# Query turns tile by tile, and an earlier, more spread image chain, in a fused attention and ReGLU kernel

## The chip, the cores and the metric

The kernel runs on one core of a Trainium2 chip. The metric is the device time of one execution in microseconds (us), taken as the median of several runs. The core has a matrix engine (TensorE, PE in the profile; its weight loads are PEld), three engines for element work (VectorE = DVE, ScalarE = ACT, GpSimd = POOL), and a sequencer that mostly issues transfers (SyncE = SP). Each engine works its own instructions in order.

## The reference

Attention over a spatially reduced image, followed by a gated feed-forward layer. There are 4 batches of 12288 queries, C = 128 channels, and an image of 384 x 32 pixels per batch, which is averaged in 4 x 4 blocks to 768 keys. Keys and values are the same numbers.

```python
kv_pool = kv.reshape(B, H // r, r, W // r, r, C).mean(axis=(2, 4))   # r = 4
k = v = kv_pool.reshape(B, -1, C) @ w_sr                             # 768 x 128 per batch
s = (q @ k.transpose(0, 2, 1)) / np.sqrt(C)
a = np.exp(s - s.max(-1, keepdims=True))
a /= a.sum(-1, keepdims=True) + 1e-09
x = (a @ v).reshape(B * N, C)
gate = np.maximum(x @ w_gate, 0.0)                                   # d_ff = 1536
out = (gate * (x @ w_val)) @ w_out
```

All inputs and the output are float32; the kernel computes in fp16 with sums in float32.

## The kernel before

The 49152 queries are cut into 96 tiles of 512. Four tiles make a group (24 groups), 24 tiles make a batch. After an opening that does the scores of tiles 0 to 3 in a special order, a loop runs over k = 4 to 98. In step k the kernel works on several tiles at once: the scores of tile k (`score_block`, `exp_block`), the values of tile k - 2 (`values`, `keep_values`), the two hidden projections of tile k - 3 (`value_proj`, `gate_proj`), and the output projection of tile k - 4 (`out_proj`, `out_turn`). The order inside a step is written out by hand as a list of words (`STEADY` and its fellows); nothing is reordered later. In what follows "tile k" is also the name of the loop's step k.

In a step of the steady state TensorE has 8 score matmuls, 6 value matmuls (L399) and 36 matmuls of the feed-forward part. The exponentials of a tile are made by ScalarE in four pieces of 128 queries (L362). They come out with queries on the partitions, but the value matmul wants keys there, so each piece is turned by a transposing transfer, `a_turn` (L389), into the tile `aT`, issued on SP right after its exponential in the word order. Step k + 2 reads it. Four `aT` tiles exist.

Queries are loaded by group on POOL's queue (`q_load`, four transfers with a cast to fp16, into one of two `q16` buffers) and turned by one transposing transfer of 16 blocks on SP (`q_turn`, L154) into one of three `qT` buffers. With ph = k % 4, both stand at ph = 1: the turn of group g + 1 and then the load of group g + 2. An older function, `q_turn_tile` (L193), turns one tile alone (4 blocks) and is used in the opening.

Keys and values of batches 1 to 3 are made while the batch before is computed, by `image_step` and three words of the list. The 768 keys come in three pairs of 128-key chunks. For each pair, with `since` counted in steps:

- four loads of image lines on SP, two per step (`kv_load`, L223, 512 KB each, two buffers `kv_in`),
- the block sums on POOL, one half of the pair per step (`pool_pixels`, L233 to L241),
- the word `tb`: a block turn on VectorE, its store to DRAM on SP (L321), and in the same step four reads from there on SP (L712), which wait for the store to land,
- the words `P` and `pk`: the projection with w_sr on TensorE and the kept keys on VectorE,
- two transposing transfers on SP, which make the values from the keys (`turn_values_dma`, L332).

A pair starts four steps after the one before.

Output stores are issued alternately on POOL's and SP's queue in the step after `out_turn` (L736): four transfers per tile, but sixteen small ones per tile for the first group, which are issued in steps 5 to 8.

So SP's queue holds, in program order: the `aT` turns, the query turns, half of the output stores, the image loads, the block store and reads, and the value turns. A transfer that has to wait for something holds up all that stand behind it.

Of the kernel before, what the change touches and what calls it, by code (L numbers as in the profile page):

```python
# [10 lines left out]
FP16 = mybir.dt.float16  # L11
# [5 lines left out]
def kernel(  # L17
# [23 lines left out]
    nc = tc.nc  # L41

    B, N, C = q.shape
# [8 lines left out]
    NS = T // 128  # L52
    NST = N // T
    NT = B * NST
    GRP = 4
# [45 lines left out]
    work = ctx.enter_context(tc.tile_pool(name="work", bufs=2))  # L101
# [19 lines left out]
    q16s, qTs, q32s, q_banks = {}, {}, {}, {}  # L121
# [11 lines left out]
    def q_load(g):  # L133
        if not 0 <= g < NG:
            return
        b, n0 = divmod(g * GRP * T, N)
        q16 = work.tile([128, GRP * NS, C], FP16, tag="q16", bufs=2)
        rows = q[b, n0 : n0 + GRP * T, :]
        if g == NG - 1:
            nc.gpsimd.dma_start(q16, rows.rearrange("(p s) c -> p s c", p=128))  # L140
        else:
            rows = rows.rearrange("(i t j s) c -> j t i s c", i=GRP, t=32, s=NS)
            for j in range(4):
                nc.gpsimd.dma_start(  # L144
                    q16[32 * j : 32 * (j + 1)].rearrange("t (i s) c -> t i s c", i=GRP), rows[j]
                )
        q16s[g] = q16

    def q_turn(g):
        if not 0 <= g < NG:  # L150
            return
        q16 = q16s.pop(g)
        qT = work.tile([128, GRP * NS, 128], FP16, tag="qT", bufs=3)
        nc.sync.dma_start_transpose(qT, q16.rearrange("p s c -> p (s c)"))  # L154
        qTs[g] = qT

    def q_load_pair(i):
        q32 = work.tile([128, 2, NS, C], FP32, tag="kv_s2", bufs=2, name="q32")
# [44 lines left out]
    kv16 = const.tile([128, B, NJC, 2 * C + 16], FP16)  # L203
    kv_in = {}

    def kv_load(b, pair, lines=range(r), queues=(nc.sync,)):
        if (b, pair) not in kv_in:
            if (b, pair) == (0, NJC // 2 - 1):
                kv_in[b, pair] = [
                    work.tile([128, NS * J // 2], FP32, tag="a16", bufs=4, name="kv_line")[  # L210
                        :, 0 : 2 * r * C
                    ].rearrange("p (h dw c) -> p h dw c", h=2, dw=r)
                    for dh in range(r)
                ]
            else:
                lines_in = work.tile([128, r, 2, r, C], FP32, tag="kv_in", bufs=2, name="kv_in")
                kv_in[b, pair] = [lines_in[:, dh] for dh in range(r)]
        parts = kv_in[b, pair]
        rows = kv[b, pair * 2 * HC : (pair + 1) * 2 * HC].rearrange(
            "(hp dh) (wp h dw) c -> dh hp wp (h dw c)", dh=r, h=2, dw=r  # L220
        )
        for dh in lines:
            queues[dh % len(queues)].dma_start(  # L223
                parts[dh].rearrange("p h dw c -> p (h dw c)"), rows[dh]
            )
# [3 lines left out]
    def pool_pixels(eng, b, pair, h):  # L229
        parts = kv_in[b, pair]  # L230
        s2 = work.tile([128, 2, r, C], FP32, tag="kv_s2", bufs=2)
        for i in range(2):
            eng.tensor_tensor(s2[:, i], parts[2 * i][:, h], parts[2 * i + 1][:, h], op=ALU.add)  # L233
        s1 = work.tile([128, r, C], FP32, tag="kv_s1", bufs=2)
        eng.tensor_tensor(s1, s2[:, 0], s2[:, 1], op=ALU.add)
        c2 = work.tile([128, 2, C], FP32, tag="kv_c2", bufs=2)
        eng.tensor_tensor(c2, s1[:, 0:2], s1[:, 2:4], op=ALU.add)
        if h == 0:
            s3s[b, pair] = work.tile([128, 4, 2, 32], FP32, tag="kv_s3", bufs=2, name="kv_s3")
        c4 = c2.rearrange("p i (j c) -> p i j c", c=32)  # L240
        eng.tensor_tensor(s3s[b, pair][:, :, h], c4[:, 0], c4[:, 1], op=ALU.add)  # L241
# [85 lines left out]
            for j in range(4)  # L327
        ]

    def turn_values_dma(b, pair):  # L330
        for jc in (2 * pair, 2 * pair + 1):
            nc.sync.dma_start_transpose(kv16[:, b, jc, C : 2 * C], kv16[:, b, jc, 0:C])  # L332


    aTs, x_banks, x16s, xTs, rinvs = {}, {}, {}, {}, {}
    hTs, o_banks, o_sbs, vals = {}, {}, {}, {}
# [41 lines left out]
    def spread_scales(k, j):  # L378
        if j == 0:
            scales[k // 2] = work.tile([128, 2, NS * 4], FP32, tag="scale", bufs=3, name="scale")  # L380
        to = scales[k // 2].rearrange("t e (s j) -> t e s j", j=4)
        for b in range(4):
            nc.gpsimd.tensor_copy(  # L383
                to[32 * b : 32 * (b + 1), :, :, j], squares[k // 2][32 * j : 32 * (j + 1)]
            )
# [99 lines left out]
    def out_proj(k, fb):  # L485
        if k >= NT - 3:
            if fb == 0:
                o_banks[k] = bank([128, NS, 128])
            for s in range(NS):
                out_add(k, fb, s, o_banks[k][:, s, :], fb == 0 and s == 0)  # L490
            return
        if fb == 0:
            o_banks[k] = bank([128, T])
        nc.tensor.matmul(  # L494
            o_banks[k], wo16[:, fb, :], hTs[k][:, fb, :], start=fb == 0, stop=fb == NFB - 1
        )
# [205 lines left out]
    out_moves, moves, spread = [], [], []  # L702

    def image_step(b, at, step):
        for pair in range(NJC // 2):
            since = at - 4 * pair
            if since in (0, 1) and step in (2, 8):
                kv_load(b, pair, [2 * since + step // 8])
            elif since in (2, 3) and step == 3:
                pool_pixels(nc.gpsimd, b, pair, since - 2)  # L710
            elif since == 5 and moves and step > 4:
                nc.sync.dma_start(*moves.pop())  # L712
            elif since == 8 and step == 1:
                turn_values_dma(b, pair)

    last = NT + LAG - 1
    for k in range(LEAD, last + 1):
        g, ph = divmod(k, GRP)
        if k == GRP:
            nc.sync.dma_start_transpose(  # L720
                qTs[1][:, 2 * NS :], q16s.pop(1)[:, 2 * NS :].rearrange("p s c -> p (s c)")
            )
        if ph == 1:
            q_turn(g + 1)
            q_load(g + 2)
        b = k // NST + 1
        at = k % NST - 6
        kO, kF, kV = k - LAG - 1, k - LAG, k - 2
        words = FIRST if kV < LEAD else STEADY if k < NT else DRAIN if k < last else LAST
        for word in words:  # L730
            head, n = word.rstrip("0123456789"), int(word.lstrip("abcdefghijklmnopqrstuvwxyzADPT") or 0)
            if head == "o":
                out_proj(kO, n)
                for queue in (nc.gpsimd, nc.sync):
                    if out_moves and n >= 2:
                        queue.dma_start(*out_moves.pop())  # L736
                if spread:
                    spread_scales(*spread.pop(0))
                if b < B:
                    image_step(b, at, n)  # L740
            elif head == "oT":
                if kO < NT - 3:
                    out_moves = out_turn(kO)
                elif k < last:
                    out_scale(kO, nc.vector, slice(0, NS))
                    out_store(kO, slice(0, NS))
            elif head in ("v", "y", "g", "h"):
                if kF < NT:
                    {"v": value_proj, "y": keep_value, "g": gate_proj, "h": gated}[head](kF, n)
            elif head in ("s", "e"):  # L750
                if k < NT:
                    {"s": score_block, "e": exp_block}[head](k, n)
                    if head == "e":
                        a_turn(k, n, n + 1)
            elif head == "r":
                if LEAD < k <= NT and k % 2 == 0:
                    invert(k - 2)
                    spread += [(k - 2, j) for j in range(4)]
            elif head in ("tb", "P", "pk"):
                pair, since = divmod(at - 5 if head == "tb" else at - 7, 4)  # L760
                if b < B and 0 <= pair < NJC // 2 and since == 0:
                    if head == "tb":
                        moves.extend(turn_blocks(b, pair))
                    elif head == "P":
                        project(b, pair)
                    else:
                        keep_projected(b, pair)
            elif LEAD <= kV < NT:
                if head == "x":
                    values(kV, n)  # L770
                else:
                    keep_values(kV)
# [33 lines left out]
```

The softmax here doesn't subtract the row's maximum and nothing guards it: scores larger than these inputs give would overflow.

## Time and profile before

| What | us |
| --- | --- |
| median of 5 runs | 1035.7 |
| lowest and highest run | 1033.78, 1037.03 |
| the profiled execution: its time | 1034.61 |
| the profiled execution: its span | 1032.8 |
| PE busy | 1022.4 |
| ACT busy | 921.0 |
| DVE busy | 862.7 |
| POOL busy | 524.5 |

The mean granted clock of the profiled execution is 0.997. The profile is of one execution: the span runs from its first to its last instruction, and its time is 1.8 us longer. Matmuls are pipelined, so PE's busy time counts overlapping instructions once. In a timeline line the first number is the start in us from the span's start, the second the length, then the engine (SPq is SP's queue of transfers, where the length is the time that issuing took, not the time until the data landed), the source line, the operation and the tiles (written<-read). In brackets stands the idle time of the engine before it, and what ended it. A line of the waits reads: who waited, for whom, us in total, times, longest.

### The profile page before, as it was taken

What the parts mean: (1) busy time and instruction counts of PE and PEld (TensorE: products, weight loads), DVE (VectorE), ACT (ScalarE), POOL (GpSimd) and SP (SyncE); (2) the same over time, 40 slices, a digit from 0 to 9 for tenths busy, and PEclk for the clock granted to TensorE, in tenths of its full rate; (3) what the DMA queues carried; (4) which work ended last, traced back from release to release, by engine and by line L of the source; (5) the groups of instructions that cost most, each with busy time, mean ns of one, the idle gap of its engine ahead of it and who ended that gap; (6) DMA issues with size and microseconds to landing.
All of it is one profiled execution on the core that took longest, in us unless ns stands there. A gap on an engine that the chain in (4) does not pass through costs nothing.

```text
span 1032.8 us, 18011 instructions
## 1 busy us (share of the span) xinstructions
PE 1022.4 (99%) x5048; PEld 490.0 (47%) x5048; DVE 862.7 (84%) x1432; ACT 921.0 (89%) x1931; POOL 524.5 (51%) x1308
## 2 busy tenths in 40 slices
PE   9999998999999999999999999999999999999998
PEld 5444443444444444444444444444444444444445
DVE  2888887788888888888888888888888888888888
ACT  5999997799999999998999999989899999999986
POOL 3576473843544656565433666566343543343332
PEclk9999999899999999999999999999999999999999
DMA  9998998997979989898888898997996876856541
GB/s 329 129 162 156 172 169 176 138 157 130 154 128 198 154 173 166 154 140 145 139 146 143 183 185 152 180 139 130 148 161 123 138 122 127 143 105 120 103 85 45
DMA packets 480500, 153.55 MB, mean 149 GB/s; under 512 B 456720, under 2 KB 470544, under 8 KB 480400
## 3 DMA queue, kind: packets, MB, share of 16 engines
q1 hardware_dynamic: 458368, 126.10, 67.0%
q0 software_dynamic: 21600, 25.19, 15.8%
q10 hardware_dynamic: 432, 1.11, 0.3%
q8 instruction: 40, 0.66, 0.3%
q14 instruction: 60, 0.49, 0.2%
HBM read 53.94 MB, written 26.35 MB: 78 GB/s over the span
## 4 chain that ended last, share of the span: by engine, by line
PE 96%; DMA 2%; ACT 1%; DVE 0%; issue 0%; SPq 0%; DVEq 0%
PE bank_ps L453 24%; PE bank_ps L466 24%; PE bank_ps L494 23%; PE bank_ps L399 12%; PE wide_ps L357 11%; DMA aT<-a 1%; DMA q<-in_q_dram 1%; PE bank_ps L480 1%; PE bank_ps L342 1%; PE bank_ps L416 1%; PE wide_ps L298 0%; PE bank_ps L266 0%; DVE hT L474 0%; ACT a L362 0%; PE bank_ps L280 0%
## 5 line engine op out<-in xcount | busy, mean ns | idle before, releaser
L474 DVE SCALAR_TENSOR_TENSOR hT<-bank_ps,val 128x512 f16<-128x512 f32 x1152 | 728.7, 680 | 110.4 <-PE bank_ps L466 88.8
L460 ACT CAST val<-bank_ps 128x512 f16<-128x512 f32 x1149 | 628.8, 596 | 46.9 <-PE bank_ps L453 26.7
L453 PE MATMUL bank_ps<-xT,wv 128*128 128x512 f16 x1152 | 421.2, 380 | 0.0
L466 PE MATMUL bank_ps<-xT,wg 128*128 128x512 f16 x1152 | 376.4, 379 | 0.0
L494 PE MATMUL bank_ps<-hT,wo 128*128 128x512 f16 x1116 | 348.4, 379 | 0.0
L362 ACT ACTIVATE a<-wide_ps 128x768 f16<-128x768 f32 x368 | 302.0, 821 | 49.8 <-PE wide_ps L357 49.7
L399 PE MATMUL bank_ps<-aT,kv 128*128 128x512 f16 x552 | 180.3, 382 | 5.2 <-DMA aT<-a 4.8
L357 PE MATMUL wide_ps<-kv,qT 128*128 128x512 f16 x736 | 180.1, 326 | 0.1
L494 PEld LDWEIGHTS <-wo 128*128 128x128 f16 x1116 | 109.2, 98 | 131.7 <-issue 0.3
L466 PEld LDWEIGHTS <-wg 128*128 128x128 f16 x1152 | 112.8, 98 | 121.9
L453 PEld LDWEIGHTS <-wv 128*128 128x128 f16 x1152 | 112.9, 98 | 106.2 <-issue 2.2
L507 POOL TENSOR_TENSOR o_sb<-o_t,scale 128x512 f32<-128x512 f32 x89 | 93.4, 1049 | 134.5 <-issue 119.2
L383 POOL COPY scale<-square 32x8 f32<-32x8 f32 x736 | 141.4, 192 | 28.6
L736 POOL DMA_DIRECT2D out_dram<-o_sb x216 | 134.7, 627 | 18.8 <-POOL o_sb L507 13.0
L357 PEld LDWEIGHTS <-qT 128*128 128x128 f16 x736 | 72.1, 98 | 87.5 <-issue 0.9
L376 POOL TENSOR_TENSOR square<-inverse 128x8 f32<-128x8 f32 x46 | 9.5, 206 | 202.0 <-DVE inverse L374 202.0
L407 DVE CAST xT<-bank_ps 128x512 f16<-128x512 f32 x92 | 63.6, 692 | 34.1 <-PE bank_ps L399 34.1
L399 PEld LDWEIGHTS <-kv 128*128 128x128 f16 x552 | 54.3, 98 | 72.6 <-DMA aT<-a 6.6
L233 POOL TENSOR_TENSOR s<-kv_in 128x512 f32<-128x512 f32 x36 | 45.5, 1272 | 74.7 <-DMA kv_in<-in_kv_dram 74.0
L362 ACT ACTIVATION_READ_ACCUMULATOR a<-wide_ps 128x1 f32 x368 | 75.9, 206 | 0.0
L502 DVE STREAM_TRANSPOSE o_t<-bank_ps 128x512 f32<-128x512 f32 x93 | 65.5, 704 | 0.0
L144 POOL DMA_DIRECT2D q<-in_q_dram x84 | 46.7, 574 | 0.4 <-PE bank_ps L494 0.4
(78 smaller groups left out, 205.2 us busy)
## 6 DMA issues: line engine op xcount, KB each, us to landing
kv_in<-in_kv_dram SPq DMA_DIRECT2D x42, 512.0 KB, 4.6
out_dram<-o_sb SPq DMA_DIRECT2D x177, 64.0 KB, 2.2
out_dram<-o_sb POOLq DMA_DIRECT2D x176, 64.0 KB, 3.2
q<-in_q_dram POOLq DMA_DIRECT2D x84, 128.0 KB, 5.5
aT<-a SPq DMA_TRANSPOSE x368, 3.4
kv_line<-in_kv_dram SPq DMA_DIRECT2D x4, 512.0 KB, 9.7
placed<-blocks SPq DMA_DIRECT2D x9, 128.0 KB, 3.4
kvT<-placed SPq DMA_DIRECT2D x36, 32.0 KB, 1.9
```

The costliest lines, as they stand in the source:

```text
L357: nc.tensor.matmul(s_ps[:, j0 * 128 : j1 * 128], qT, kv16[:, b, j0:j1, 0:C], start=True, stop=True)
L362: nc.scalar.activation(a16s[k][:, s, :], s_banks.pop(s)[:, 0:J], AF.Exp, scale=qk_scale, accum_out=a_sums[k // 2][:, k % 2, s : s + 1],)
L383: nc.gpsimd.tensor_copy(to[32 * b : 32 * (b + 1), :, :, j], squares[k // 2][32 * j : 32 * (j + 1)])
L399: nc.tensor.matmul(x_banks[k], kv16[:, k // NST, jc, C : 2 * C], aT[:, jc], start=first, stop=x_left[k] == 0,)
L453: nc.tensor.matmul(proj_banks["v", k, fb], wv16[:, fb * 128 : (fb + 1) * 128], xTs[k], start=True, stop=True,)
L460: (nc.vector.tensor_copy if k < LEAD - 1 and fb == 5 else nc.scalar.copy)(vals[k, fb], freed(proj_banks.pop(("v", k, fb))))
L466: nc.tensor.matmul(proj_banks["g", k, fb], wg16[:, fb * 128 : (fb + 1) * 128], xTs[k], start=True, stop=True,)
L474: nc.vector.scalar_tensor_tensor(hTs[k][:, fb, :], freed(proj_banks.pop(("g", k, fb))), 0.0, vals.pop((k, fb)), op0=ALU.max, op1=ALU.mult,)
L494: nc.tensor.matmul(o_banks[k], wo16[:, fb, :], hTs[k][:, fb, :], start=fb == 0, stop=fb == NFB - 1)
L502: nc.vector.transpose(o_t, freed(o_banks.pop(k)))
L507: nc.gpsimd.tensor_tensor(to, o_by, scale.to_broadcast([128, NS, 4, 32]), op=ALU.mult)
L736: queue.dma_start(*out_moves.pop())
```

## The change

Four edits.

1. `q_turn` takes a tile number i and turns only that tile's 4 blocks. The first three tiles of group g + 1 are turned at ph = 1, 2 and 3 of group g, the last at ph = 0 of its own group, each at the start of the step. The load of group g + 2 stays at ph = 1; its buffer is that of group g, whose last part is now read by the turn issued one step before.
2. The image chain begins two steps sooner: `at` is k % 24 - 4 instead of - 6.
3. Within the chain, the sums come at since 3 and 4 instead of 2 and 3, the reads and `tb` at 6 instead of 5, `P` and `pk` at 8 instead of 7. With the sooner begin, the loads stand two steps earlier than before and all of these one step earlier.
4. The two value turns of a pair stand at since 9 and 11, one each, instead of both at 8.

The same instructions are issued as before, except that each query turn of 16 blocks has become four of 4 blocks.

```diff
-    def q_turn(g):
+    def q_turn(g, i):
         if not 0 <= g < NG:
             return
-        q16 = q16s.pop(g)
-        qT = work.tile([128, GRP * NS, 128], FP16, tag="qT", bufs=3)
-        nc.sync.dma_start_transpose(qT, q16.rearrange("p s c -> p (s c)"))
-        qTs[g] = qT
+        if g not in qTs:
+            qTs[g] = work.tile([128, GRP * NS, 128], FP16, tag="qT", bufs=3, name="qT")
+        at = slice(i * NS, (i + 1) * NS)
+        nc.sync.dma_start_transpose(
+            qTs[g][:, at], q16s[g][:, at].rearrange("p s c -> p (s c)")
+        )
+        if i == GRP - 1:
+            del q16s[g]
...
-    def turn_values_dma(b, pair):
-        for jc in (2 * pair, 2 * pair + 1):
-            nc.sync.dma_start_transpose(kv16[:, b, jc, C : 2 * C], kv16[:, b, jc, 0:C])
+    def turn_values_dma(b, jc):
+        nc.sync.dma_start_transpose(kv16[:, b, jc, C : 2 * C], kv16[:, b, jc, 0:C])
...
             since = at - 4 * pair
             if since in (0, 1) and step in (2, 8):
                 kv_load(b, pair, [2 * since + step // 8])
-            elif since in (2, 3) and step == 3:
-                pool_pixels(nc.gpsimd, b, pair, since - 2)
-            elif since == 5 and moves and step > 4:
+            elif since in (3, 4) and step == 3:
+                pool_pixels(nc.gpsimd, b, pair, since - 3)
+            elif since == 6 and moves and step > 4:
                 nc.sync.dma_start(*moves.pop())
-            elif since == 8 and step == 1:
-                turn_values_dma(b, pair)
+            elif since in (9, 11) and step == 1:
+                turn_values_dma(b, 2 * pair + since // 11)
...
+        if ph == 0 and g > 1:
+            q_turn(g, GRP - 1)
+        elif ph > 0:
+            q_turn(g + 1, ph - 1)
         if ph == 1:
-            q_turn(g + 1)
             q_load(g + 2)
         b = k // NST + 1
-        at = k % NST - 6
+        at = k % NST - 4
...
-                pair, since = divmod(at - 5 if head == "tb" else at - 7, 4)
+                pair, since = divmod(at - 6 if head == "tb" else at - 8, 4)
```

## The prediction

> **What bounds the kernel now.** I read the page's busy times first, then PE's waits, then the timelines around the longest wait.
>
> ```profile
> PE 1022.4 (99%) x5048; PEld 490.0 (47%) x5048; DVE 862.7 (84%) x1432; ACT 921.0 (89%) x1931; POOL 524.5 (51%) x1308
> ```
>
> TensorE is at work for 99% of the span, and the change removes no matmul. So it can only win back idle TensorE time, or add some. The waits of PE after the opening are these:
>
> ```profile
> PE bank_ps L399 <- DMA aT<-a: 4.8, 2, 4.3
> PE bank_ps L399 <- DVE o_t L502: 0.4, 1, 0.4
> ```
>
> Three waits, all in front of the value matmuls (L399), which read the turned weights aT. The longest in PE's timeline, with the granted clock around it in the windows view (PEclk is the column behind POOL's):
>
> ```profile
> 175.86 0.38 PE L453 MATMUL bank_ps<-xT,wv 128*128 128x512 f16 x1
> 180.54 0.59 PE L399 MATMUL bank_ps<-aT,kv 128*128 128x512 f16 x1 [4.30 <-DMA aT<-a]
> ...
> 176.00:179.60 3.60, 0.24 (x2) 0.00 (x0) 1.21 (x2) 0.79 (x2) 1.12 (x1) 1.00 1.15 212
> 179.60:186.40 6.80, 5.86 (x15) 2.63 (x16) 2.08 (x3) 2.40 (x5) 6.48 (x13) 0.50 0.87 153
> 186.40:196.80 10.40, 10.40 (x52) 4.87 (x51) 8.57 (x15) 8.89 (x20) 9.55 (x22) 1.00 1.24 158
> ```
>
> TensorE stands still from 176.24 to 180.54, and the clock is at half for 6.8 us from 179.6 on. What the tile paid is read from DVE's output turn (L502), one per tile:
>
> ```profile
> 165.52 0.69 DVE L502 STREAM_TRANSPOSE o_t<-bank_ps 128x512 f32<-128x512 f32 x1
> 175.92 0.72 DVE L502 STREAM_TRANSPOSE o_t<-bank_ps 128x512 f32<-128x512 f32 x1
> 194.10 0.69 DVE L502 STREAM_TRANSPOSE o_t<-bank_ps 128x512 f32<-128x512 f32 x1
> ```
>
> A tile takes 10.37 (10.34 and 10.39 in turn), 10.82 where an image pair is projected. This one took 194.10 - 175.92 = 18.18, so 7.36 too much. The two small ones (475.22 to 486.62, 725.86 to 737.32) took 11.40 and 11.46, 0.6 too much each. All other tiles run at TensorE's pace. **The change can win 7.36 + 0.59 + 0.64 = 8.6 us, and no more.**
>
> Why aT was late is in SP's timeline, since SP issues every turn in order:
>
> ```profile
> 165.68 0.56 SPq L321 DMA_DIRECT2D placed<-blocks  x1
> 169.33 0.79 SPq L712 DMA_DIRECT2D kvT<-placed  x2
> 170.21 2.50 SPq L389 DMA_TRANSPOSE aT<-a  x1
> 172.76 1.03 SPq L712 DMA_DIRECT2D kvT<-placed  x2
> 173.83 0.62 SPq L223 DMA_DIRECT2D kv_in<-in_kv_dram  x1
> 174.55 4.29 SPq L389 DMA_TRANSPOSE aT<-a  x3
> ```
>
> These are tile 15's turns. Its exponentials ended at 150.5 to 157.1 (ACT's timeline), so the last turn was issued 18.7 us late. SP is a queue with a backlog, and here it also stands 3.0 us for the block store to land (166.3 to 169.3). The lag of each tile's first aT turn behind its exponential, tiles 8 to 16: 6.6, 12.5, 9.1, 7.9, 12.5, 13.0, 10.1, 10.8, 16.5. It begins in tiles 5 to 8, where SP has eight small stores a tile. By tile 27 it is gone.
>
> **The change, part by part, in SP's time.** A tile's cost is the time between the first aT turns of two tiles. Tile 9 has four turns and two stores: 100.38 to 107.35, 7.0; tile 13 the same, 7.9; I take 7.2. Two image loads: tile 10, 107.35 to 116.50, leaves 1.9. The block chain (store, wait, four reads): tile 11, 116.50 to 131.49, leaves 5.9. A value turn is 1.2 (row L332, median 1223 ns). The whole query turn:
>
> ```profile
> L154 SPq DMA_TRANSPOSE qT<-q x22: 1840/4851/6672, 47.5 to 927.2; - x22
> L193 SPq DMA_TRANSPOSE qT<-q x2: 1199/1264/1328, 27.7 to 31.4; - x2
> ```
>
> It held SP 6.7, 4.0 and 5.4 us ahead of tiles 9, 13 and 17. One tile's turn is the opening's L193: 1.25. Four are 5.0, so the split saves SP nothing; it only spreads the 5.
>
> Image loads move from tiles 6/7, 10/11, 14/15 to 4/5, 8/9, 12/13; the chain from 11, 15, 19 to 10, 14, 18; value turns from pairs in 14, 18, 22 to single ones in 13 to 23. Tile 8's first turn: before 6.6 late; plus four quarters (5.2 with the queue's gaps) less the whole turn of tile 5 (1.9), less two loads (1.3, since those now in tile 4 meet an idle SP): 8.6. Then each tile adds its items less 10.37. Tile 8 cost 16.3, of which 6.7 was the query turn: 9.6 + 1.25 + 1.9 = 12.75, lag 11.0. Tile 9: 7.2 + 1.25 + 1.9 = 10.35, lag 11.0. Tile 10: 7.2 + 1.25 + 5.9 = 14.35, lag 15.0. Tile 11: 8.45, lag 13.1. Tile 12: 10.35, 13.1. Tile 13 (loads and a value turn): 11.55, 14.3. Tile 14 (chain): 14.35, 18.3. Then 9.65, 8.45, 9.65 bring it to 17.6, 15.7, 15.0 at tile 18.
>
> The last turn's lag is the first's less 0.8 in a plain tile (tiles 9 and 12: less 1.0 and 1.2; tile 13: 0), plus the chain. Lag of the last turn plus what was to spare at L399 came to 12.0 to 16.6 in tiles 8 to 14, mean 14.6. So to spare after the change: tile 10, 14.6 - (11.0 - 0.8 + 5.9) = -1.5; tile 14, 14.6 - (14.3 + 5.1) = -4.8; tile 18, 14.6 - (15.0 + 5.1) = -5.5. TensorE waits 1.5, then 3.3 more, then 0.7 more: 5.5 instead of 4.3, but in pieces. By the ends of that spread the sum is 3.5 to 8.1. For tile 15 of before the same reckoning gives -3.2 where 4.3 was waited: it errs by 1 us, to the short side.
>
> Does the clock fall? Waits of 0.43 and 0.47 (475 and 726 us) left it alone; 4.30 brought it down, 3.37 after TensorE stopped, for 6.83 at half: 3.4 lost. The pieces of 1.5 and 0.7 are nearest to the small waits: nothing. The piece of 3.3 lies between, nearest to the long one, but it would end just before the 3.37 at which the clock fell: I take no fall, and keep 3.4 for a rival. The Trainium skill (TensorE: Matmul & The Clock Gate, section "What's actually happening") has the clock halved only after an idle window of about 3.4 us and restored after as much work. Its windows run freely, so by that rule even 4.3 us need not fall; by rule alone all three pieces are free and the sum stays as below.
>
> Late batches start from lag 0 (tile 27); their four busiest tiles hold the same items before and after (28.8 + 5 + 3.8 + 5.9 + 2.4 = 45.9 in 41.5). Of the two waits of 0.6 none or all may stay: I take half, 0.6.
>
> On other queues: POOL's image sums begin one tile earlier but one tile longer after their loads, so most of POOL's 74.0 us of waiting for kv_in goes; it is hidden (POOL is 51% busy). New is that the query load of phase 1 waits for the last quarter, issued at phase 0 behind SP's lag; behind it on POOL stand two stores and the next output scaling. That is at most 5 to 8 us in tile 13, against two tiles until the o_t buffer is wanted: nothing. DVE's block turn comes two tiles after the sums, as before: nothing. One thing speaks against the change: the loads now stand in phases 0 and 1, where the query load runs. aT turns issued 1.2 us ahead of that load took 5 to 7 us to land instead of 2.8. The skill (DMA: Bandwidth & Descriptors, section "Issuing engines are not separate DMA queues") says that SP's and POOL's transfers interleave on the same 16 engines; by it the meeting costs whatever both queues hold. That price is not in the 5.5.
>
> **Sum**, against the profiled execution (span 1032.8, its time 1034.61): 1034.6 - 8.6 + 5.5 + 0.6 = 1032.1. The median of the runs is 1.1 higher, so **1033.2**, with 1031 to 1036 for this case alone.
>
> **The rivals.**
> *Slower:* loads meet the query load in tiles 9 and 13, 1.5 us each (half of 2.8 to 5.8). Waits become 3.0 in tile 10, 4.8 in tile 14, 0.7 later: 8.5, and the clock falls once or twice. Once: 1035.7 - 8.6 + 8.5 + 3.4 = 1039.0; twice 1042.4. It decides as soon as waits plus 3.4 per fall exceed 8.6 + 2.1 = 10.7. For it: the lag is inherited from tile 8, which the change makes 2.0 worse. Against: the chain's tiles are freed of loads.
> *Same:* waits as forecast, but the 3.3 trips the clock: 1035.7 - 8.6 + 5.5 + 0.6 + 3.4 = 1036.6.
> *All of it won:* what follows a whole query turn lands late (the turns after it at 5 to 6 us), and that goes with the split; lags stay under 14 and no wait is left: 1027.1. Against: the quarters still move the same bytes.
>
> **How the numbers follow.** About 0.2%, 2 us, is what a measurement of this kernel can tell from no change. Forecast 0.36 (of it 0.25 faster, 0.09 same, 0.02 slower), clock tripped 0.17 (0.13 same, 0.04 slower), slower 0.33, all won 0.14. Together 0.39, 0.22, 0.39: the sign is open, since waits are moved rather than removed. The range runs from all won, 1027.5, to between one and two falls, 1041.5.
>
> **What would show it.** Right: L399 waits in tiles 10, 14 and 18, each under 3.4 us, clock at 1.00, tile 15 free. Wrong: half clock in the windows of tiles 10 to 14 (slower), or no L399 wait at all (all won). SP's lag at tile 8 should be near 8.6 and at tile 15 near 18 less what TensorE waited; a lag under 12 there sinks the ledger.

## The result, and the profile after

The changed kernel takes 1038.8 us (median of 22 runs, 1034.0 to 1045.3) where the kernel before, run beside it, takes 1035.2 (41 runs): a ratio of 1.0036 (95% interval 1.0023 to 1.0049), so **3.7 us slower**. Run once more on another chip it was 6.5 us slower (experiment 1). The forecast was 1033.2. The profiled execution took 1034.81 (span 1032.9), which is among the fastest of its 22, so its waits show the kind of loss and not its usual size.

The page's busy times, and the shares of the chain that ended last:

```profile
PE 1020.3 (99%) x5048; PEld 488.4 (47%) x5048; DVE 863.4 (84%) x1432; ACT 919.8 (89%) x1931; POOL 525.7 (51%) x1308
...
PE 91%; DMA 6%; ACT 1%; DVE 1%; issue 0%; SPq 0%; DVEq 0%
```

TensorE still bounds the kernel, but 6% of the chain are now transfers (2% before). PE's waits, at the value matmul, which has become L401, and POOL's new wait, ahead of the query load (L144) for the last quarter of the turn:

```profile
PE bank_ps L401 <- DMA aT<-a: 4.5, 6, 1.6
PE bank_ps L401 <- DVE hT L476: 1.0, 1, 1.0
PE bank_ps L401 <- DVE o_t L504: 0.4, 1, 0.4
POOL q L144 <- DMA qT<-q: 58.9, 10, 9.9
```

Three waits, the longest of 4.3 us, have become eight small ones, in tiles 8, 10, 12, 13, 14, 16, 20 and 68, together 5.9 us. The first and longest, in PE's timeline and in SP's:

```profile
103.51 0.38 PE L455 MATMUL bank_ps<-xT,wv 128*128 128x512 f16 x1
105.47 0.38 PE L401 MATMUL bank_ps<-aT,kv 128*128 128x512 f16 x1 [1.58 <-DMA aT<-a]
```

```profile
97.88 3.45 SPq L391 DMA_TRANSPOSE aT<-a  x2
101.52 1.90 SPq L155 DMA_TRANSPOSE qT<-q  x1
103.51 1.24 SPq L391 DMA_TRANSPOSE aT<-a  x1
```

TensorE waits for a turn that SP issued at 103.51, behind a quarter of a query turn. The clock stayed at 1.00; tile 15, where the kernel before lost 7.4 us, is whole. The quarters in the rows of the query turn (least, median and greatest issue time in ns):

```profile
L155 SPq DMA_TRANSPOSE qT<-q x88: 1188/1260/2311, 48.1 to 957.9; - x88
```

A figure that can be compared over kernels is the stretch from the first to the last output turn of DVE. Before it took 964.1 us, of which 8.6 could be won, so its floor is 955.5. In the changed kernel it took 962.9: the 8.6 us of before are won, and 7.4 us are lost in other places.

### The profile page after: what moved, and what is told of

The parts are those of the page before. It is cut to its first block, busy times and chain, and to the rows that moved or that the text cites. A ratio compares the mean times of both kernels' runs of the same rounds, so it can differ in the third digit from the quotient of the medians.

```text
span 1032.9 us, 18121 instructions
## 1 busy us (share of the span) xinstructions
PE 1020.3 (99%) x5048; PEld 488.4 (47%) x5048; DVE 863.4 (84%) x1432; ACT 919.8 (89%) x1931; POOL 525.7 (51%) x1308
## 4 chain that ended last, share of the span: by engine, by line
PE 91%; DMA 6%; ACT 1%; DVE 1%; issue 0%; SPq 0%; DVEq 0%
PE bank_ps L455 23%; PE bank_ps L468 23%; PE bank_ps L496 21%; PE bank_ps L401 11%; PE wide_ps L359 11%; DMA aT<-a 3%; DMA kv_line<-in_kv_dram 1%; DVE hT L476 1%; DMA kv_in<-in_kv_dram 1%; ACT a L364 1%; PE bank_ps L482 1%; ACT val L462 1%; DMA out_dram<-o_sb 0%; PE bank_ps L418 0%; PE wide_ps L302 0%
## 5 line engine op out<-in xcount | busy, mean ns | idle before, releaser
L401 PE MATMUL bank_ps<-aT,kv 128*128 128x512 f16 x552 | 179.0, 379 | 5.9 <-DMA aT<-a 4.5
L401 PEld LDWEIGHTS <-kv 128*128 128x128 f16 x552 | 53.9, 98 | 74.1 <-issue 10.1
L144 POOL DMA_DIRECT2D q<-in_q_dram x84 | 46.7, 573 | 74.0 <-DMA qT<-q 58.9
```

The source lines that it names most:

```text
L401: nc.tensor.matmul(x_banks[k], kv16[:, k // NST, jc, C : 2 * C], aT[:, jc], start=first, stop=x_left[k] == 0,)
```

## The experiments

All were run beside the kernel before, on the same chip. "Against before" is the ratio less one, times 1035.7. The lag is what the prediction's ledger counts: how far a tile's first `aT` turn is issued behind its exponential, averaged over tiles 8 to 20 and 36 to 46. SP's issue time is the sum over all its transfers. Lags and sums are of one profiled execution each. The kernels of experiments 1 to 4 ran on one chip, and so did those of 5 to 8, 9 to 12 and 13 to 16. Two kernels were run on two chips: their figures against before lie 2.8 us (changed) and 4.3 us (spread alone) apart, so smaller differences between chips say little.

| Kernel | Median us | Ratio (95%) | Against before | Lag 8-20 | Lag 36-46 | SP issue time |
| --- | --- | --- | --- | --- | --- | --- |
| before | 1035.7 | 1 | 0 | 11.2 | 8.2 | 817 |
| changed | 1038.8 | 1.0036 (1.0023, 1.0049) | +3.7 | 14.2 | 11.0 | 860 |
| 1 changed, again | 1041.2 | 1.0063 (1.0042, 1.0083) | +6.5 | 13.9 | 12.5 | 873 |
| 2 split alone | 1036.9 | 1.0019 (1.0001, 1.0037) | +2.0 | 11.8 | 8.7 | 851 |
| 3 chain alone (sooner and spread) | 1031.0 | 0.9952 (0.9935, 0.9970) | -5.0 | 11.4 | 6.9 | 836 |
| 4 changed, query load at ph 3 | 1037.2 | 1.0019 (1.0006, 1.0032) | +2.0 | 13.3 | 9.9 | 840 |
| 5 chain, four quarters in a row | 1044.4 | 1.0078 (1.0050, 1.0106) | +8.1 | 12.8 | 12.1 | 872 |
| 6 chain, query load at ph 3 | 1035.4 | 0.9997 (0.9980, 1.0014) | -0.3 | 10.8 | 1.3 | 789 |
| 7 changed, three query buffers | 1038.7 | 1.0023 (1.0003, 1.0042) | +2.4 | 13.7 | 10.9 | 868 |
| 8 chain, moves on POOL | 1027.9 | 0.9919 (0.9899, 0.9939) | -8.4 | 7.3 | 1.2 | 818 |
| 9 chain, two halves in a row | 1033.5 | 0.9965 (0.9945, 0.9985) | -3.6 | 11.5 | 9.0 | 835 |
| 10 changed, moves on POOL | 1028.9 | 0.9922 (0.9897, 0.9946) | -8.1 | 10.0 | 0.2 | 828 |
| 11 spread alone | 1029.0 | 0.9912 (0.9884, 0.9940) | -9.1 | 9.9 | 2.4 | 809 |
| 12 sooner alone | 1056.4 | 1.0163 (1.0122, 1.0204) | +16.9 | 10.9 | 8.7 | 838 |
| 13 spread alone, again | 1029.4 | 0.9954 (0.9934, 0.9973) | -4.8 | 8.9 | 2.7 | 803 |
| 14 spread and split | 1028.5 | 0.9944 (0.9927, 0.9961) | -5.8 | 10.3 | 5.5 | 834 |
| 15 spread, query load at ph 3 | 1030.6 | 0.9962 (0.9947, 0.9977) | -3.9 | 9.7 | 1.5 | 791 |
| 16 spread, moves on POOL | 1027.0 | 0.9927 (0.9910, 0.9945) | -7.6 | 6.5 | 0.6 | 797 |

The theory first held was that the early chain costs (image loads beside the query load) and that the split costs nothing. Its rival was that the split costs.

**1. The changed kernel again**, without an edit, since its profiled execution had been one of its fastest.

> The changed kernel once more, unedited, for another profiled execution: its median is 1038.8 us in runs from 1034 to 1045, but the one profiled execution took 1034.8, with 5.9 us of waits at the value matmul in pieces of 0.3 to 1.6 us and no clock fall. Thin margins (my theory): the same tiles (8, 10, 12, 13, 14, 16, and late ones such as 40 or 68) wait again, longer, 8 to 13 us in all, most of it without a clock fall. Clock theory: the waits stay near 6 us and one or two falls of 3.4 us make up the rest.

1041.2. This profiled execution was the slowest of its runs (1045.9), so it shows the other end. Its waits at L401, over the whole span and from 250 us on:

```profile
PE bank_ps L401 <- DMA aT<-a: 12.6, 9, 2.2
...
PE bank_ps L401 <- DVE hT L476: 2.2, 2, 1.2
```

```profile
PE bank_ps L401 <- DMA aT<-a: 5.3, 4, 1.9
PE bank_ps L401 <- DVE hT L476: 1.1, 1, 1.1
```

14.8 us in all, 6.4 of them in the late batches, where the kernel before lost 0.9. The clock was at half once, for 3.41 us, which loses 1.7. So it is many waits, not falls of the clock. The stretch of output turns took 974.1, 18.6 over the floor; waits and clock make 16.5 of it. The usual run lies between the two profiles.

**2. The split alone** (quarters; image chain as before).

```diff
-        if ph == 1:
-            q_turn(g + 1)
+        if ph == 0 and g > 1:
+            q_turn(g, GRP - 1)
+        elif ph > 0:
+            q_turn(g + 1, ph - 1)
```

> Only the query turn is split into one per tile; the image chain stands where it stood before. Early-chain theory: the split is not the cause, the lag at tile 8 stays near 8 and the time is that of the kernel before, 1033 to 1036. Split theory (four issues of 1.26 us cost SP more than one whole turn, and the query load waits for the last quarter): the time is that of the changed kernel, 1038 to 1040, and SP's lag no longer drains to 0 between the batches.

+2.0 us, just outside no change, and between the two forecasts. SP's issue time rises from 817 to 851, and the value matmul (L403 here) waits longer than before:

```profile
PE bank_ps L403 <- DMA aT<-a: 9.0, 4, 3.8
```

**3. The chain alone** (sooner and spread; the whole query turn at ph 1).

```diff
-        at = k % NST - 6
+        at = k % NST - 4
...
-            elif since == 8 and step == 1:
-                turn_values_dma(b, pair)
+            elif since in (9, 11) and step == 1:
+                turn_values_dma(b, 2 * pair + since // 11)
```

> Only the image chain is moved and spread; the query turn is one transfer of 16 blocks at phase 1 as before. Early-chain theory: slower like the changed kernel or more, 1038 to 1042, with the longest waits in tiles 10 and 14. Split theory: the time of the kernel before, 1034 to 1037. If both parts matter, it lies between.

5 us *faster* than before. The waits of its PE (value matmul at L397 here), and the query turn:

```profile
PE bank_ps L397 <- DMA aT<-a: 3.4, 2, 2.2
```

```profile
L154 SPq DMA_TRANSPOSE qT<-q x22: 1869/4133/9542, 48.5 to 925.4; - x22
```

The first theory falls: the chain is no loss, the quarters on top of it are, together with what they do to the query load. From 3 to 1, on one chip, they cost 10 us.

**4. The changed kernel with the query load two steps later.**

```diff
-        if ph == 1:
+        if ph == 3:
             q_load(g + 2)
```

> The changed kernel with the query load at phase 3 instead of phase 1, away from the image loads (phases 0 and 1) and long after the last quarter turn. Collision theory (image loads and query load share the DMA engines in tiles 9, 13, 29 and so on): 2 to 4 us back, 1034 to 1037, POOL's 58.9 us of waiting for qT gone. Early-chain and split theories: 1038 to 1040, since POOL's wait is hidden and the bytes are the same.

4 us better than experiment 1 on the same chip: POOL's wait for the last quarter is gone. It does not reach experiment 3.

**5. The chain with four quarters in a row at ph 1**, which takes POOL's wait and the spreading away and leaves the number of turns.

```diff
-        nc.sync.dma_start_transpose(qT, q16.rearrange("p s c -> p (s c)"))
+        for i in range(GRP):
+            at = slice(i * NS, (i + 1) * NS)
+            nc.sync.dma_start_transpose(qT[:, at], q16[:, at].rearrange("p s c -> p (s c)"))
```

> The moved image chain with the query turn issued as four quarters, but all four in a row in phase 1, where the whole turn stood. The query load behind it waits for no later tile. Issue-count theory: each transposing DMA holds SP some 1.2 to 1.6 us whatever its size, so four in a row hold SP 5.5 to 6.5 us, where the whole turn of the moved chain alone held it 2.7 to 4.7; SP's lag drains more slowly, late batches start from a lag of 2 to 4 us, and value-matmul waits come back: 1036 to 1038 (moved chain alone: 1031.0). Rival, position: what costs is that POOL's query load waits for the last quarter and then runs beside the image loads of the next tiles; with the quarters in a row that is gone, and the time is within 1.5 of 1031.0, with POOL's wait for the query turn under 10 us in all.

1044.4, worse than either theory said, and 13 us above the whole turn. PE's waits for the turns, against experiment 3's 3.4:

```profile
PE bank_ps L399 <- DMA aT<-a: 14.4, 9, 4.3
```

POOL's wait for the last quarter is not there in this kernel, so the number of turns costs without it. SP's issue time goes from 836 to 872, as with the quarters of experiment 1 (873).

**6. The chain with the query load at ph 3**, on experiment 3.

```diff
         if ph == 1:
             q_turn(g + 1)
+        if ph == 3:
             q_load(g + 2)
```

> The moved image chain with the whole query turn in phase 1 as before, and the query load put from phase 1 to phase 3. No wait on the query turn is to be taken away here (it was issued two tiles earlier), so what changes is only beside what the load runs: the image loads now stand in phases 0 and 1. Collision theory: the late load frees the image loads, aT turns land sooner, 1027 to 1029.5 against 1031.0 for the moved chain alone. POOL-wait theory: without a wait to remove nothing is won, 1030 to 1032; and as the late load then runs beside the block store and its reads, the SP wait for the store comes back from 13.4 to some 25 us.

No gain: 4.7 us above experiment 3. Both theories miss. In the late batches the load at ph 3 does relieve SP: its lag there is 1.3 and no value matmul waits. In the first batch SP's backlog carries the image loads of tile 13 along until they meet the query load all the same (issued at 148.99 and 152.81, the query load at 150.61 to 152.27). The `aT` turns issued from 151.1 to 156.0 then took 9 to 11 us to land, where 2.7 is the least, and TensorE stood still for 5.7. So loads that meet do cost; what phase they meet in depends on how late SP is.

**7. The changed kernel with three `q16` buffers**, so that the load at ph 1 need not wait for the last quarter.

```diff
-        q16 = work.tile([128, GRP * NS, C], FP16, tag="q16", bufs=2)
+        q16 = work.tile([128, GRP * NS, C], FP16, tag="q16", bufs=3)
...
-            q16s[g] = work.tile([128, GRP * NS, C], FP16, tag="q16", bufs=2, name="q16")
+            q16s[g] = work.tile([128, GRP * NS, C], FP16, tag="q16", bufs=3, name="q16")
```

> The changed kernel with three buffers for the loaded queries instead of two, so that the query load of phase 1 need not wait for the last quarter of the turn. It stays in phase 1. POOL-wait theory: the delayed load is what the move to phase 3 cured, so this is as good: 1036 to 1038.5, against 1041.2 for the changed kernel. Collision theory: the load still runs beside the image loads, so 1040 to 1042, though POOL's wait for the query turn (58.9 us) is gone. Issue-count theory: the four quarters still hold SP, so neither reaches the 1031.0 of the moved chain alone.

Between the two forecasts. The interval touches those of both runs of the changed kernel: POOL's wait is worth 1 to 4 us by the ratios, and no more can be said.

**8. The chain with the block store and its reads on POOL's queue.**

```diff
-        nc.sync.dma_start(placed, blocks.rearrange("p j h c -> p (j h c)"))
+        nc.gpsimd.dma_start(placed, blocks.rearrange("p j h c -> p (j h c)"))
...
-                nc.sync.dma_start(*moves.pop())
+                nc.gpsimd.dma_start(*moves.pop())
```

> The moved image chain with whole query turns, and the block store and its four reads issued on POOL's queue instead of SP's. If SP's issue time is what the waits of the value matmul come from, this takes up to 5.9 us per image pair off it (store 0.6, standing for its landing 2, reads 2 to 3), the two remaining waits (3.4 us and a clock fall of 3.4) go, and the time is 1025 to 1028. If POOL is then what is late (its output scalings stand behind the landing of the store and behind the loads), waits for o_t or for the query turn appear, and the time is 1031 to 1036.

1027.9, as the theory of SP's time says; one value-matmul wait of 0.9 us is left. That theory was then put to two tests, 9 and 10.

**9. Two halves in a row**, on experiment 3.

```diff
-        nc.sync.dma_start_transpose(qT, q16.rearrange("p s c -> p (s c)"))
+        for i in range(2):
+            at = slice(2 * i * NS, 2 * (i + 1) * NS)
+            nc.sync.dma_start_transpose(qT[:, at], q16[:, at].rearrange("p s c -> p (s c)"))
```

> The moved image chain with the query turn in two halves, one behind the other in phase 1. Number-of-issues theory: the price grows with the number of transposing DMAs in which the same 128 KB go, so one gives 1031.0, four in a row gave 1044.4, and two should lie between, at 1033 to 1039, with SP's lag in tiles 40 to 48 between those of the two. Threshold theory: what costs is that a small transfer is landed in another order, or that anything less than the whole turn hands the rings to the next item earlier; then two cost like four, 1042 to 1045, or like one, 1030 to 1032.

1.4 us above the whole turn by the ratios, with intervals that overlap, where four in a row cost 13. So the price does not grow evenly with the number: SP's issue time is that of the whole turn (835 against 836). In the traces the shortest issue of a whole turn is 1.87 us (experiment 3), of a half 1.23, of a quarter 1.19 (5); their means are 4.6, 2.4 and 1.5. Two halves take as long as the whole, four quarters some 30% more (132 us in the run against 102). By these least times an estimate of what the pieces must cost is 4 x 1.19 = 4.8 us for four quarters, already more than the whole turn's mean, and 2.5 us for two halves. (The expectation's 128 KB is one quarter; the whole turn moves 512.)

**10. The changed kernel with the block moves on POOL.**

```diff
-        nc.sync.dma_start(placed, blocks.rearrange("p j h c -> p (j h c)"))
+        nc.gpsimd.dma_start(placed, blocks.rearrange("p j h c -> p (j h c)"))
...
-                nc.sync.dma_start(*moves.pop())
+                nc.gpsimd.dma_start(*moves.pop())
```

> The changed kernel, quarters and all, with the block store and its four reads on POOL's queue instead of SP's. SP-time theory: the quarters cost only because SP has no time to spare in tiles 8 to 20, 36 to 46 and 60 to 70; with some 5 us per image pair taken off SP they are nearly free, 1028 to 1031, within 3 us of the same kernel with whole turns (1027.9). Rival: the quarters cost through the DMA engines or through POOL's late query load, which this does not relieve (POOL has more to issue): 10 us more than with whole turns, 1036 to 1040.

This is the sharpest test, since it keeps the quarters and the early chain and takes only the block moves off SP, and the loss is gone: 8 us faster than before, level with experiment 8. Its only wait of the value matmul for a turn, and what is left of POOL's wait for the last quarter:

```profile
PE bank_ps L401 <- DMA aT<-a: 1.9, 1, 1.9
...
POOL q L144 <- DMA qT<-q: 11.1, 3, 6.3
```

So the quarters cost where SP has no time left for them; where it has, they are nearly free. The expectation took it that the late query load would stay as it was. It did not: with SP on time the last quarter is issued sooner, and POOL's wait falls from 58.9 us to 11.1. So this run does not tell SP's own lateness from the query load that is late because of it. Experiment 5 has quarters without the late load and loses 13 us; experiment 14 below has the late load, away from the image loads, and loses nothing.

**11 to 13. Sooner and spread taken apart**, with whole query turns. 11 and 13 are one kernel: the new steps, begun where the chain was. Its last pair takes both value turns at since 9, since 11 would fall out of the batch. Against experiment 3:

```diff
-        at = k % NST - 4
+        at = k % NST - 6
...
                 turn_values_dma(b, 2 * pair + since // 11)
+                if pair == NJC // 2 - 1:
+                    turn_values_dma(b, 2 * pair + 1)
```

> Whole query turns; the image chain begun where it was, with its steps spread over more tiles as in the changed kernel: image sums and block moves one tile later, value turns singly. If the gain of the moved chain comes from spreading (one value turn a tile, the chain's moves apart from the loads), 1030 to 1033. If it comes from beginning sooner, so that the block store no longer stands beside the image loads and the query turn, the time is that of the kernel before or worse, 1034 to 1040, and SP's wait for the store stays above 20 us (13.4 with the moved chain, 23.6 before).

> The kernel with the chain's steps spread and nothing else changed, once more, as the base of the next three on the same chip. It gave 8 us less than the kernel before; 5 to 11 us less again, unless that figure was drawn low. Theory: it wins because the block moves and value turns no longer stand together, with the image loads where they were.

12 is the kernel before with one edit:

```diff
-        at = k % NST - 6
+        at = k % NST - 4
```

> Whole query turns; the image chain begun two tiles sooner, with its steps where they were relative to the loads. If beginning sooner is the gain, 1030 to 1033 and SP's wait for the store near 13 us. If it comes from spreading, 1034 to 1038, with the two value turns in one tile again just ahead of a chain, and a value-matmul wait in tile 16 or 20.

The gain is the spreading: 9.1 and 4.8 us in two runs (their intervals overlap a little), with SP's lag in tiles 36 to 46 down from 8.2 to 2.4 and 2.7. It is not sure in every execution: the profiled one of experiment 11, the slowest of its six, has one wait of the value matmul and the half clock for 6.8 us after it:

```profile
PE bank_ps L397 <- DMA aT<-a: 5.2, 1, 5.2
```

Beginning sooner without the spreading costs 17 us, which is worse than either forecast. The value matmul's waits in 12, and those of POOL's image sums for the image loads, which were 74.0 us before:

```profile
PE bank_ps L399 <- DMA aT<-a: 23.9, 6, 6.4
...
POOL s L233 <- DMA kv_in<-in_kv_dram: 119.2, 12, 17.3
```

The sums stand one tile behind loads that land late, and POOL also has the query loads. That this is what makes the turns late is likely and not shown. The spread steps put the sums a tile later, and experiments 11 and 13 have no such wait of the sums. With spread steps, beginning sooner costs 0 to 4 us (3 against 13 and 11). It is not what made the change slow by itself.

**14. Spread and split, begun where it was.** Against the changed kernel:

```diff
-        at = k % NST - 4
+        at = k % NST - 6
...
                 turn_values_dma(b, 2 * pair + since // 11)
+                if pair == NJC // 2 - 1:
+                    turn_values_dma(b, 2 * pair + 1)
```

> The changed kernel with the chain begun where it was before: spread steps and quarters, image loads in the tiles of phases 2 and 3 again. Theory now: the quarters cost SP some time in every group, but what made it 10 us was their meeting with the image loads in phases 0 and 1 and with a query load that waits for the last quarter; so this lies 1 to 4 us above the spread kernel, and below the kernel before. Rival, the quarters alone: they cost the same 8 to 13 us wherever the chain stands, and this lies at or above the kernel before.

5.8 us faster than before, 0.9 under experiment 13 on the same chip, where 1 to 4 above was expected; the rival is refuted too. So the quarters cost nothing that can be measured here, though SP's issue time rises as always, from 803 to 834, and though POOL still waits for the last quarter. The value matmul's waits in 14, and POOL's:

```profile
PE bank_ps L401 <- DMA aT<-a: 0.7, 1, 0.7
...
PE bank_ps L401 <- DVE o_t L504: 0.5, 1, 0.5
...
POOL q L144 <- DMA qT<-q: 34.3, 8, 8.4
```

**15. Spread with the query load at ph 3**, to bring query load and image loads together from the other side. Against 13:

```diff
         if ph == 1:
             q_turn(g + 1)
+        if ph == 3:
             q_load(g + 2)
```

> The spread kernel with the query load moved from phase 1 to phase 3, into the tiles where the image loads stand. Collision theory: what the sooner chain cost was the image loads beside the query load, so bringing the two together from the other side costs as much: 3 to 6 us above the spread kernel, the query load's last transfer landing 8 us or more after its issue where it took some 5.7, and SP's lag in tiles 29 and 33 at 6 us instead of 2.5. Rival, that beginning sooner is bad in itself (it meets the backlog left over from the opening): the phase of the query load makes no odds, within 1.5 us of the spread kernel.

1.2 us above 13, intervals overlapping: the rival of that expectation holds, and the lag in tiles 29 and 33 was 0.5 and 1.4, not 6. What did change is the whole turn itself, in 13 and in 15:

```profile
L154 SPq DMA_TRANSPOSE qT<-q x22: 1802/4384/6216, 48.0 to 921.0; - x22
```

```profile
L154 SPq DMA_TRANSPOSE qT<-q x22: 1324/2717/3889, 47.7 to 924.1; - x22
```

So of the 4 to 5 us for which a whole turn holds SP, over a third goes with the query load issued beside it.

**16. Spread, with the block moves on POOL**, the version to which all this points. Against 13:

```diff
-        nc.sync.dma_start(placed, blocks.rearrange("p j h c -> p (j h c)"))
+        nc.gpsimd.dma_start(placed, blocks.rearrange("p j h c -> p (j h c)"))
...
-                nc.sync.dma_start(*moves.pop())
+                nc.gpsimd.dma_start(*moves.pop())
```

> The spread kernel with the block store and its reads on POOL's queue. The kernel before has 8.6 us to win in all, and the spread kernel has won about 8 of them, so little is left: the time is within 2 us of the spread kernel and not under 1026 on a chip where the kernel before takes 1035.7. If POOL becomes late with its output scalings, 2 to 4 us more.

**1027.0, in runs from 1026.6 to 1027.1: 8.1 us under the kernel before by the medians**, and 2.4 under experiment 13, a little more than was expected. No value matmul waits any more; PE's longest waits are now

```profile
PE bank_ps L611 <- POOL ident masks.py:199: 1.4, 1, 1.4
PE bank_ps L280 <- ACT kvT_chunk L126: 0.4, 1, 0.4
```

and both lie in the opening. The stretch of output turns is 955.4, which is the floor.

## Why the prediction was wrong, by its steps

- *"The change can win 8.6 us, and no more"*: right. Experiment 16 has reached it.
- *"Four are 5.0, so the split saves SP nothing; it only spreads the 5"*: **this step failed.** In the changed kernel four quarters held SP 4 x 1.39 = 5.6 us, in experiment 1 4 x 1.47 = 5.9, where the whole turn's mean over the run was 4.5 before and 4.6 in experiment 3; the prediction compared 5.0 with the longer turns of tiles 9, 13 and 17 (mean 5.4). With the quarters SP's issue time rose by 34 us (before to 2), 30 (13 to 14) and 36 (3 to 1), and the sum over the query turns alone by 26, 35 and 27. That is some 1.5 us in each of the 22 groups, a term that the ledger set at nothing.
- *"Late batches start from lag 0 ... the same items before and after"*, 0.6 us: failed with it. The lag at tile 28 was 2.1 (3.4 in experiment 1, 0 before and in 3), and in tiles 36 to 46 it stood at 11.0 and 12.5 (8.2 before). The late batches lost 0.4 us in the first profile and 6.4 in that of experiment 1.
- *The ledger of the first batch* held in the main. First-turn lags, forecast against the two profiles: tile 8 8.6 (9.9, 9.0); tile 10 11.0 (14.8, 14.8); tile 11 15.0 (15.7, 13.1); tile 13 13.1 (14.3, 14.5); tile 15 18.3 less waits (16.2, 16.6); tile 18 15.0 (13.4, 13.1). It was worst at tiles 9 and 10, 11.0 forecast for both and 14.6 to 14.9 found: tile 8, where image loads and query load meet, took SP longer than its items. That price the prediction named and left out of its sum. (Its reading of that price is loose: in the kernel before, the `aT` turns issued up to 0.7 us ahead of a query load took 4.3 to 7.1 us to land, and one 0.85 us ahead took 2.8.) 5.5 us of waits were forecast, and 5.5 came in the first batch of the first profile, but in seven tiles instead of three: with 0 to 3 us to spare in every tile, each small delay of a run becomes a wait. Experiment 1's first batch lost 8.4.
- *No fall of the clock*: right in the first profile. In experiment 1 a wait of 2.2 us brought one, below the 3.37 that was taken as the point, but it lost 1.7 and not 3.4. A fall goes by the idle share of one window (the last section), not by the length of a wait.
- *POOL's query load behind the last quarter: nothing*: wrong on the early chain. It waited ten times, up to 9.9 us. Experiment 4 gives 4 us back by moving the load, 7 some of it by a third buffer. In experiment 14 it waits eight times and nothing is lost.
- *The rivals*: "slower" named 1039.0, by waits past 10.7 and one fall of the clock. The median lies there, in part by luck. In experiment 1 waits and clock made 16.5, and the wait in tile 8 is where loads and query load meet; but most of it has a cause that the rival did not name, the quarters: without them, and with the same loads meeting, experiment 3 is 10 us faster. That the chain's new steps are worth 5 to 9 us was in no case of the prediction, so that the change was taken as one thing, where it is a gain, and two costs that are small on that gain one at a time and large together.

**Why together.** The lag of tiles 8 to 20 in the table sorts nearly all kernels: 6.5 to 10.3 where 3.9 to 9.1 us are won, 10.8 to 11.5 in 6, in the kernel before and in 3 and 9, 11.8 to 14.2 in all that lose; 12 is apart, with a wait of its own. By the prediction's reckoning the value matmul has 12.0 to 16.6 us of slack behind an exponential. Work on SP that keeps its lag under that cost nothing in 14; at the edge of it, as in tiles 8 to 20 of the changed kernel, delays became waits. Sooner (803 or 809 to 836) and split (30 to 36) take about as much of SP's time, but not in the same way. The split adds it in the query turns themselves. Sooner adds no transfer: the same `aT` turns held SP 512 us in 3 where they held it 487 and 494 in 13 and 11, and the query turns 102 where it was 90 and 91. One of the two on top of the spread chain costs 0 to 4 us, both together 9 to 16, and when the block moves go to POOL both are nearly free again (10). The Trainium skill (DMA: Bandwidth & Descriptors, section "Issuing engines are not separate DMA queues") has it that issuing from several engines saves only the sequencer's time to start a transfer, usually small beside the transfer itself. Here it was not small in its effect: the block moves took 24 us of SP's issue time in the changed kernel, and SP stood 12.9 us more for the stores to land; taking both off SP was worth 12 to 15 us (10 against the two runs of the changed kernel).

**Open.** How the cost of the quarters on the early chain divides between SP's own time and the late query load (4 and 7 give back up to 4 us; 5, without the late load, still costs 13; 10 relieves both). Whether the turns that hold SP longer on the early chain are held by the load of the DMA engines: the median turn lands no later in the changed kernel (3.3 us after its issue, 3.4 before), but single turns beside both loads take 9 to 11, as in 6. And why quarters in a row lose so much more than halves, beyond the least times above.

## What to carry to other kernels

Where one queue issues nearly all transfers, add up its issue time and measure how late it runs against the slack of its readers: well below the slack an added transfer cost nothing here, at the edge delays became waits, and two edits that were nearly harmless one at a time were not so together. Cutting a transfer into pieces can be paid at the issuing queue: here a piece of a quarter took at least 1.19 us to issue, and the whole 1.32. Before judging a change of several edits, price each edit alone and on top of the others: here one alone was the gain. Moving five small transfers per image pair to an idler queue was worth 2 to 4 us on the two chains with whole turns (13 to 16, 3 to 8), and 12 to 15 on the changed kernel, whose queue ran latest.

## What was not expected of the hardware

**A clock fall follows one window, not the length of a wait.** In the records of the granted clock every stretch, full or half, but the last of a profile is a whole number of 3.413 us long (177.49 = 52 x 3.413 and 846.51 = 248 x 3.413 in experiment 3). On that grid the windows of experiments 3 and 2 read so (start:end, length, busy time of PE, PEld, DVE, ACT and POOL, granted clock, DMA share, GB/s):

```profile
179.10:182.50 3.40, 1.24 (x7) 0.61 (x7) 1.51 (x3) 0.83 (x3) 2.33 (x3) 1.00 1.18 221
182.50:186.00 3.50, 3.50 (x11) 1.24 (x9) 1.59 (x3) 2.11 (x5) 0.00 (x0) 0.51 1.00 164
```

```profile
174.80:178.20 3.40, 1.60 (x8) 0.52 (x6) 2.57 (x5) 2.15 (x5) 0.00 (x0) 1.00 0.82 192
178.20:181.60 3.40, 1.36 (x7) 0.71 (x8) 0.66 (x1) 0.41 (x1) 2.67 (x3) 1.00 0.93 185
181.60:185.00 3.40, 3.40 (x18) 1.75 (x17) 2.74 (x6) 2.77 (x7) 3.32 (x7) 1.00 0.72 137
```

In experiment 3 a wait of 2.2 us fell into one window, and the next ran at half. In experiment 2 a wait of 3.8 us lay across a border, 1.60 and 1.36 us of work stayed in the two windows, and the clock held. Over all profiles of this study a fall followed each of the 14 full-clock windows in which PE was idle for 63% or more, and none of those with 59% or less (the kernels' ends, after the last matmuls, left out). The Trainium skill (TensorE: Matmul & The Clock Gate, section "What's actually happening") gives the free-running window of 3413 ns, which the grid shows, and a fall after an idle window; the runs add that the window need not be wholly idle.

**The least time to issue a transposing transfer hardly depends on its size**: 1.19 us for 128 KB (experiment 5), 1.23 for 256 KB (9), 1.32 for 512 KB (15). Above that it stretched: means were 1.5 us for 128 KB (5), 2.4 for 256 KB (9) and 2.5 to 5.4 for 512 KB (15, 8), and the large one's median fell from 4.4 (13) to 2.7 (15) when the query load was no longer issued beside it.
